# VectorE's share of a softmax exp: one fp16 number from four operations, or a sum of two from three

## The chip, the cores and the metric

The kernel runs on one core of a Trainium2 chip. Times are device microseconds (us) of one execution. The engines are PE (TensorE), ACT (ScalarE), DVE (VectorE) and POOL (GpSimd); "PEld" is PE's weight load.

## The reference, cut to what matters

The program does two independent attention blocks, A (linear attention) and B (full softmax attention), each with S = 2048, D = 512, 32 heads of 16. B is the heavy one:

```
q, k, v = split(x @ wqkv)                   # 32 heads of 16
p = softmax(q @ k.T * 0.25)                 # 32 x 2048 x 2048 exps
o = p @ v
out_b = merge_heads(o) @ wo
```

The kernel works on P transposed (keys on partitions, queries along the columns). It cuts the 32 x 2048 x 2048 scores into 2048 "blocks" of 128 partitions by 512 columns of work for one instruction. V has a column of ones, so the denominators come out of the same product. There are 32 "units" of 64 blocks; a unit is 512 queries of four heads.

## The kernel before

A planner in Python places every instruction before the program is emitted. It knows an assumed duration for each and decides block by block whether ScalarE or VectorE makes the exp. ScalarE reads scores from five PSUM banks (PSUM is where TensorE leaves its results) in turns of 3 and 2 blocks:

```python
# ScalarE: exp of 3 or 2 blocks, PSUM -> fp16                    (L810)
sch.add("act", lambda e: e.activation(PT[:, row, c0:c0 + w], SCR[sl][:, 0:w], ACTF.Exp, scale=SC), ...)
# TensorE refills those banks: QK (q times k) with 32 rows, four row groups   (L664)
e.matmul(dst, lhsT=KM[32*g:32*g+32, ...], rhs=QT[32*g:32*g+32, ...], tile_position=(32*g, 0))
```

VectorE has two further PSUM banks, pD, which it shares with all other work of the kernel. It scales a block and writes it as int16, so that the bits, read as fp16, are 2^n(1+f), a line between powers of two. Then four operations over a group of four blocks correct the mantissa:

```python
DG, NDG = 4, 4              # blocks in a group, groups in flight
DI = sb("DI", [128, NDG, DG * 512], I16);  DQ = sb("DQ", [128, 1, DG * 512], I16)
e.tensor_scalar(DI[...], DB[...], ESC, EB, op0=mult, op1=add)        # L750, 1 block, out of PSUM
tensor_scalar(Dq,  I,   0x200, 6, bitwise_xor, logical_shift_left)   # L866, 2048 columns
tensor_tensor(Dqb, Dq,  Dq,  mult)                                   # L867
tensor_scalar(Dqh, Dqb, EC, EO, mult, add)                           # L868
tensor_tensor(I,   I,   Dqh, add)                                    # L869
```

TensorE multiplies finished blocks with V (L923). These products have 17 output rows and four column groups; the planner charges them so:

```python
while len(bt) < PVB and any(byg.values()): ...     # PVB = 8 blocks at most in a batch
dur = 0.13 + 0.085 * len(bt)                       # the planner's duration, us
e.matmul(PVb[32*g:32*g+17, 0:512], lhsT=VV[:, j, ...], rhs=P, start=first, stop=last_, tile_position=(0, 32*g))
```

## Time and profile before

The kernel before took 831.24 us (median of 3; 829.41 to 832.32). The profiled execution took 834.9 us, longer than all of these. The head of its page, then the two lines of its costliest groups. A group line gives line, engine, operation, output and input tile, shape and count; then busy us and the mean ns of one; then the idle time just before them and what ended most of it.

```profile
span 833.1 us, 12897 instructions
## 1 busy us (share of the span) xinstructions
PE 695.8 (84%) x5406; PEld 210.7 (25%) x5406; DVE 748.5 (90%) x1153; ACT 789.1 (95%) x730; POOL 46.5 (6%) x43
...
PEclk9999999999999799998786999999988998699996
...
ACT 69%; PE 16%; DVE 14%; issue 1%; POOL 0%; POOLq 0%
...
L810 ACT ACTIVATE PT<-pS 128x1536 f16<-128x1536 f32 (+1 forms) x673 | 778.7, 1384 | 23.1 <-PE pD L664 11.2
L664 PE MATMUL pS<-QT,KM 32*128 32x512 bf16 x1682 | 277.5, 410 | 104.3 <-ACT PT L810 100.0
```

And VectorE's part of a block, from the groups kept apart by shape:

```profile
L750 DVE TENSOR_SCALAR DI<-pD 128x512 int16<-128x512 f32 x348 | 234.0, 682 | 29.3 <-PE pD L664 27.2 <-PE pS L664 0.3
L869 DVE TENSOR_TENSOR DI<-DI,DQ 128x2048 int16<-128x2048 int16 x91 | 111.3, 1223 | 1.6
L867 DVE TENSOR_TENSOR DQ<-DQ 128x2048 bf16<-128x2048 int16 x91 | 111.1, 1221 | 1.5
L866 DVE TENSOR_SCALAR DQ<-DI 128x2048 int16<-128x2048 int16 x91 | 63.6, 699 | 1.8
L868 DVE TENSOR_SCALAR DQ<-DQ 128x2048 f16<-128x2048 bf16 x91 | 62.4, 685 | 0.4
```

How to read it. ScalarE is busy 95% of the span, and most of the chain that ended last is its exp. Consecutive exps overlap in the records (the mean of one is longer than busy time over count), so the cost of a block is busy time over blocks: 778.7 / 1682 = 0.463 us. VectorE's cost of a block is 0.682 + (699 + 1221 + 685 + 1223) / 4 / 1000 = 1.64 us. Neither engine can be relieved alone: the time falls when blocks move from ScalarE to VectorE. ScalarE idles 833.1 - 789.1 = 44.0 us.

One line is PEclk, the granted clock in tenths for 40 slices. The mean was 0.924.

### The profile page before, as it was taken

How to read it: one execution, taken by the hardware profiler on the slowest of the kernel's cores; microseconds unless marked ns; L12 is line 12 of the kernel's file. 1: busy time of each engine (PE TensorE's matmuls, PEld its weight loads, DVE VectorE, ACT ScalarE, POOL GpSimd, SP SyncE). 2: the span in 40 equal slices, each digit the busy share in tenths (PEclk: the TensorE clock that was granted, in tenths of full speed). 3: DMA queues.
4: the chain of work that ended last, by engine and by line, in shares of the span. 5: the costliest groups of instructions: out<-in, count | busy, mean ns of one | idle time of the engine just before them, and what ended most of it. 6: DMA issues, size and time to landing. Idle time of an engine off the chain costs nothing.

```text
span 833.1 us, 12897 instructions
## 1 busy us (share of the span) xinstructions
PE 695.8 (84%) x5406; PEld 210.7 (25%) x5406; DVE 748.5 (90%) x1153; ACT 789.1 (95%) x730; POOL 46.5 (6%) x43
## 2 busy tenths in 40 slices
PE   7888888888888888877778889888878888888886
PEld 4322222233222222221111222222222222122222
DVE  6999899986999899899999998999999988999981
ACT  5799999999999999999999999999999999999993
POOL 2000023100000002110000001220000000000000
PEclk9999999999999799998786999999988998699996
DMA  9100000000000000000000000000000000000000
GB/s 307 48 1 24 29 1 1 1 1 1 2 1 1 1 1 1 1 1 1 1 1 1 7 14 7 1 7 14 7 1 14 14 13 13 1 20 14 20 26 29
DMA packets 13136, 13.47 MB, mean 16 GB/s; under 512 B 1808, under 2 KB 12560, under 8 KB 13072
## 3 DMA queue, kind: packets, MB, share of 16 engines
q1 hardware_dynamic: 12272, 12.19, 4.5%
q8 instruction: 44, 0.72, 0.4%
q10 hardware_dynamic: 800, 0.39, 0.2%
q14 instruction: 20, 0.16, 0.1%
HBM read 8.39 MB, written 4.19 MB: 15 GB/s over the span
## 4 chain that ended last, share of the span: by engine, by line
ACT 69%; PE 16%; DVE 14%; issue 1%; POOL 0%; POOLq 0%
ACT PT L810 67%; PE pS L664 5%; PE pPV L923 5%; DVE DI L750 4%; DVE DQ L867 2%; DVE DI L869 2%; ACT EA L534 1%; DVE DQ L866 1%; PE pD L450 1%; PE pD L947 1%; DVE DQ L868 1%; PE pD L615 1%; DVE OT L944 1%; PE pD L543 1%; PE pD L970 0%
## 5 line engine op out<-in xcount | busy, mean ns | idle before, releaser
L810 ACT ACTIVATE PT<-pS 128x1536 f16<-128x1536 f32 (+1 forms) x673 | 778.7, 1384 | 23.1 <-PE pD L664 11.2
L664 PE MATMUL pS<-QT,KM 32*128 32x512 bf16 x1682 | 277.5, 410 | 104.3 <-ACT PT L810 100.0
L750 DVE TENSOR_SCALAR DI<-pD 128x512 int16<-128x512 f32 (+1 forms) x357 | 244.9, 695 | 32.6 <-PE pD L664 30.6
L923 PE MATMUL pPV<-PT,VV 128*17 128x512 f16 x1682 | 220.9, 410 | 0.7 <-ACT PT L810 0.3
L664 PEld LDWEIGHTS pS<-QT,KM 32*128 32x128 bf16 x1682 | 64.6, 91 | 365.0 <-ACT PT L810 325.0
L664 PE MATMUL pD<-QT,KM 32*128 32x512 bf16 x366 | 142.6, 415 | 1.3 <-DVE DI L750 1.1
L869 DVE TENSOR_TENSOR DI<-DI,DQ 128x2048 int16<-128x2048 int16 x92 | 112.0, 1217 | 1.6
L867 DVE TENSOR_TENSOR DQ<-DQ 128x2048 bf16<-128x2048 int16 x92 | 111.8, 1215 | 1.5
L923 PE MATMUL pPV<-DI,VV 128*17 128x512 f16 x366 | 79.7, 425 | 3.0 <-DVE OT L944 2.4
L476 POOL TENSOR_SCALAR KM<-KR,PAR 128x512 bf16<-128x512 bf16 x24 | 41.7, 1748 | 511.3 <-DVE KR L474 511.3
L866 DVE TENSOR_SCALAR DQ<-DI 128x2048 int16<-128x2048 int16 x92 | 64.0, 696 | 1.8
L868 DVE TENSOR_SCALAR DQ<-DQ 128x2048 f16<-128x2048 bf16 x92 | 62.8, 683 | 0.4
L923 PEld LDWEIGHTS pPV<-PT,VV 128*17 128x17 bf16 x1682 | 40.8, 88 | 84.5 <-issue 75.4
L543 PE MATMUL pD<-Wa,xTa 128*128 128x256 bf16 x256 | 39.0, 283 | 4.5 <-DVE DI L750 2.8
L450 PE MATMUL pD<-xTb,Wb 128*128 128x512 bf16 x124 | 37.8, 401 | 5.7 <-DVE DI L750 2.9
L664 PEld LDWEIGHTS pD<-QT,KM 32*128 32x128 bf16 x366 | 31.9, 92 | 10.2 <-DVE DI L750 4.1
L947 PE MATMUL pD<-identf,OT 128*128 128x128 f32 x128 | 31.2, 336 | 1.9 <-DVE OT L944 1.5
L534 ACT ACTIVATE EA<-pD 128x256 bf16<-128x256 f32 (+1 forms) x48 | 30.2, 630 | 0.6 <-PE pD L564 0.6
L944 DVE COPY OT<-pPV 128x512 f32<-128x512 f32 x32 | 21.9, 684 | 8.6 <-PE pPV L923 8.5
L543 PEld LDWEIGHTS pD<-Wa,xTa 128*128 128x128 bf16 x256 | 21.2, 100 | 21.2 <-issue 7.0
L419 DVE CAST OB<-pD 128x512 bf16<-128x512 f32 x30 | 20.5, 683 | 5.2 <-PE pD L615 5.1
L923 PEld LDWEIGHTS pPV<-DI,VV 128*17 128x17 bf16 x366 | 16.3, 90 | 28.5 <-issue 12.5
(88 smaller groups left out, 376.2 us busy)
## 6 DMA issues: line engine op xcount, KB each, us to landing
out_dram<-OB SPq DMA_DIRECT2D x32, 128.0 KB, 1.7
KNa<-in_A_x_dram SPq DMA_DIRECT2D x4, 512.0 KB, 6.1
ON<-in_B_x_dram SPq DMA_DIRECT2D x3, 512.0 KB, 7.7
Wa<-in_A_wqkv_dram SPq DMA_DIRECT2D x1, 1536.0 KB, 11.9
Wb<-in_B_wqkv_dram SPq DMA_DIRECT2D x2, 384.0 KB, 8.4
Wb<-in_B_wqkv_dram SPq DMA_DIRECT2D x1, 512.0 KB, 6.8
WOb<-in_B_wo_dram SPq DMA_DIRECT2D x1, 512.0 KB, 12.0
WOa<-in_A_wo_dram SPq DMA_DIRECT2D x1, 512.0 KB, 12.1
```

The source lines that it names most:

```text
L450: return e.matmul(f32v(bk), lhsT=Wb[:, cc, kind * 512 + Gp * 128:kind * 512 + Gp * 128 + 128], rhs=xTb[:, cc, sc * 512:(sc + 1) * 512], st ...
L476: st.append(("pool", 0.7, f_op("pool", lambda e, e_=e_: e.tensor_scalar(KM[:, r, e_, cs], KR[:, kr, :], PAR[:, e_:e_ + 1], None, op0=ALU.m ...
L543: return e.matmul(f32v(bk)[:, 256 * k_:256 * k_ + 256], lhsT=xTa[:, cc, t * 128:(t + 1) * 128], rhs=Wa[:, cc, 512 + 512 * k_ + 256 * hp:51 ...
L664: return e.matmul(dst, lhsT=KM[32 * g:32 * g + 32, Gp % 2, e_, j * 128:(j + 1) * 128], rhs=QT[32 * g:32 * g + 32, Gp % 2, c * 512:(c + 1) ...
L750: sch.add("dve", lambda e: e.tensor_scalar(DI[:, buf, i * 512:(i + n) * 512], DB[:, bi * 512:(bi + n) * 512], ESC, EB, op0=ALU.mult, op1=A ...
L810: sch.add("act", lambda e: e.activation(PT[:, row, c0:c0 + w], SCR[sl][:, 0:w], ACTF.Exp, scale=SC), reads=skeys(sl), writes=[("PT", row, ...
L866: (0.07 + w * 0.00027, lambda e: e.tensor_scalar(Dq, I, 0x200, 6, op0=ALU.bitwise_xor, op1=ALU.logical_shift_left), ik, [("DQ", q)]),
L867: (0.07 + w * 0.00053, lambda e: e.tensor_tensor(Dqb, Dq, Dq, op=ALU.mult), [("DQ", q)], [("DQ", q)]),
L868: (0.07 + w * 0.00027, lambda e: e.tensor_scalar(Dqh, Dqb, EC, EO, op0=ALU.mult, op1=ALU.add), [("DQ", q)], [("DQ", q)]),
L869: (0.07 + w * 0.00053, lambda e: e.tensor_tensor(I, I, Dqh, op=ALU.add), ik + [("DQ", q)], ik)]
L923: sch.add("pe", lambda e, g=g, j=j, h=h, P=P, first=first, last_=last_: e.matmul(PVb[32 * g:32 * g + 17, 0:512], lhsT=VV[:, j, vcol(h):vco ...
L947: return e.transpose(f32v(bk)[:, qb * 128:(qb + 1) * 128], OT[:, ob, qb * 128:(qb + 1) * 128], identf[:])
```

## The change

The intent is a cheaper block on VectorE, paid on TensorE. The masked bits give two fp16 numbers, H = 2^n(1+f) times (1+f)/2, which is 2^n(1+f)^2/2, and 2^n itself (with a small constant in the mantissa). Their sum is close to a constant times 2^(n+f). The sum is never formed: both are multiplied with V, and TensorE's accumulation adds them. That is three operations on a group instead of four. Both tensors must now live until the product, so DQ grows from 4 to 15 KB a partition. With DI the two grow from 20 to 30 KB. 8 KB of that come from two buffers of the output stage, four fifths of which now lie in KNa, a tensor that A needs only for its K side. Groups become 3 blocks, 5 in flight. THRESHOLD_BITS is a bound on the scores, as float bits: above it a general softmax, whose code is not shown here, runs as well. It goes from 9.5 to 9.25.

```diff
-THRESHOLD_BITS = 0x41180000
+THRESHOLD_BITS = 0x41140000
-    DG = 4
-    NDG = 4
+    DG = 3
+    NDG = 5
-    EB = 15.0 * 1024.0 - 7.95374
-    EC = 3.30484893e-4 / 4096.0
-    EO = -79.35798
+    EB = 14754.203187
-        DQ = sb("DQ", [128, 1, DG * 512], I16)
+        DQ = sb("DQ", [128, NDG, DG * 512], I16)
-        ONT = sb("ONT", [128, 5, 512], BF)
-        OB = sb("OB", [128, 5, 512], BF)
+        ONT = sb("ONT", [128, 1, 512], BF)
+        OB = sb("OB", [128, 1, 512], BF)
 ... (out slots 1 to 4 of ONT and OB are views of KNa, after A's last K job)
-  tensor_scalar(Dq, I, 0x200, 6, bitwise_xor, logical_shift_left)
-  tensor_tensor(Dqb, Dq, Dq, mult)
-  tensor_scalar(Dqh, Dqb, EC, EO, mult, add)
-  tensor_tensor(I, I, Dqh, add)
+  tensor_scalar(Q, I, 0x3FF, 0x3800, bitwise_and, bitwise_or)
+  tensor_tensor(Qh, Ih, Qh, mult)
+  tensor_scalar(I, I, 0xFC00, 8, bitwise_and, bitwise_or)
 ... (both Qh and Ih go to the products)
-            while len(bt) < PVB and any(byg.values()):
+            while nmm < PVB and any(byg.values()):
 ...
+                        nmm += len(bt[-1][2])
-            dur = 0.13 + 0.085 * len(bt)
+            dur = 0.13 + 0.085 * nmm
 ... (within a batch, a round over the column groups with the first numbers, then with the second)
```

More of the change, by code (lines that the diff above doesn't have):

```diff
@@ L601, in bass_concat_heads__linear_attn_block__softmax_full_mha__prompt_kernel @@
         stores = []
+        KNf = KNa[:, :, :].rearrange("p (s b) n -> p s (b n)", b=2)
+        ont = lambda o2: ONT[:, 0, :] if o2 == 0 else KNf[:, o2 - 1, :]
+        obf = lambda o2: OB[:, 0, :] if o2 == 0 else KNf[:, o2 + 3, :]
+        ontk = lambda o2: [("ONT", 0)] if o2 == 0 else kst(o2 - 1)
+        obk = lambda o2: [("OB", 0)] if o2 == 0 else kst(o2 + 3)
         def otr_job(src, keys, o2, needs, gives, lane="dve", **kw):
@@ L608, in otr_job @@
             return Job([("pe", 4 * TRB, f_pe(tr, list(keys) + ["identb"])),
-                        (lane, 0.43 if lane == "dve" else 0.6, f_ev(lane, copy_to(lane, lambda: ONT[:, o2, :], lambda bk: bfv(bk, 512)), [], [("ONT", o2)]))],
-                       needs, gives, **kw)
+                        (lane, 0.43 if lane == "dve" else 0.6, f_ev(lane, copy_to(lane, lambda: ont(o2), lambda bk: bfv(bk, 512)), [], ontk(o2)))],
+                       needs + ([("akv", 1, bl) for bl in range(2)] if o2 else []), gives, **kw)
         def omm_job(ab, t, o2, needs, gives, lane="dve", **kw):
@@ L614, in mm @@
             def mm(e, bk, hb):
-                return e.matmul(f32v(bk), lhsT=ONT[:, o2, hb * 128:(hb + 1) * 128], rhs=WO[:, hb, :], start=(hb == 0), stop=(hb == 3))
+                return e.matmul(f32v(bk), lhsT=ont(o2)[:, hb * 128:(hb + 1) * 128], rhs=WO[:, hb, :], start=(hb == 0), stop=(hb == 3))
             def fin(bk):
-                sch.add(lane, lambda e: copy_to(lane, lambda: OB[:, o2, :], lambda bk: f32v(bk))(e, bk), reads=[bk[3]], writes=[("OB", o2)])
-                stores.append(sch.add(out_lanes[o2], lambda e: e.dma_start(out[0][t * 128:(t + 1) * 128, col0:col0 + 512], OB[:, o2, :]),
-                                      reads=[("OB", o2)], queue="sp", force_signal=True))
-            return Job(halves(mm, [("ONT", o2), wkey]) + [(lane, 0.7 if lane == "dve" else 0.6, fin)], needs, gives, **kw)
+                sch.add(lane, lambda e: copy_to(lane, lambda: obf(o2), lambda bk: f32v(bk))(e, bk), reads=[bk[3]], writes=obk(o2))
+                stores.append(sch.add(out_lanes[o2], lambda e: e.dma_start(out[0][t * 128:(t + 1) * 128, col0:col0 + 512], obf(o2)),
+                                      reads=obk(o2), queue="sp", force_signal=True))
+            return Job(halves(mm, ontk(o2) + [wkey]) + [(lane, 0.7 if lane == "dve" else 0.6, fin)], needs, gives, **kw)
         rem = [[list(range(NT)) for g in range(4)] for u in range(NU)]
@@ L813, in ex @@
                     for i, b in enumerate(bl):
-                        pv_ready[b[0]].append((en_ + LAT, b, PT[:, row, c0 + i * 512:c0 + (i + 1) * 512], ("PT", row, sl), (row, sl)))
+                        pv_ready[b[0]].append((en_ + LAT, b, [(PT[:, row, c0 + i * 512:c0 + (i + 1) * 512], ("PT", row, sl))], (row, sl)))
                 push("act", en + LAT, 0, d, ex)
@@ L855, in chain_next @@
                 return
-            buf, q = qwait.pop(0), qfree.pop(0)
+            buf = qwait.pop(0)
+            qfree.pop(0)
             s_ = dgroup["st"][buf]
@@ L859, in chain_next @@
             w = 512 * n
-            I = DI[:, buf, 0:w]
-            Dq = DQ[:, q, 0:w]
-            Dqb = DQ.bitcast(BF)[:, q, 0:w]
-            Dqh = DQ.bitcast(F16)[:, q, 0:w]
+            I, Q = DI[:, buf, 0:w], DQ[:, buf, 0:w]
+            Ih, Qh = DI.bitcast(F16)[:, buf, 0:w], DQ.bitcast(F16)[:, buf, 0:w]
             ik = [("DI", buf, i) for i in range(n)]
+            qk_ = [("DQ", buf)]
             ops = [
-                (0.07 + w * 0.00027, lambda e: e.tensor_scalar(Dq, I, 0x200, 6, op0=ALU.bitwise_xor, op1=ALU.logical_shift_left), ik, [("DQ", q)]),
-                (0.07 + w * 0.00053, lambda e: e.tensor_tensor(Dqb, Dq, Dq, op=ALU.mult), [("DQ", q)], [("DQ", q)]),
-                (0.07 + w * 0.00027, lambda e: e.tensor_scalar(Dqh, Dqb, EC, EO, op0=ALU.mult, op1=ALU.add), [("DQ", q)], [("DQ", q)]),
-                (0.07 + w * 0.00053, lambda e: e.tensor_tensor(I, I, Dqh, op=ALU.add), ik + [("DQ", q)], ik)]
+                (0.07 + w * 0.00027, lambda e: e.tensor_scalar(Q, I, 0x3FF, 0x3800, op0=ALU.bitwise_and, op1=ALU.bitwise_or), ik, qk_),
+                (0.07 + w * 0.00053, lambda e: e.tensor_tensor(Qh, Ih, Qh, op=ALU.mult), ik + qk_, qk_),
+                (0.07 + w * 0.00027, lambda e: e.tensor_scalar(I, I, 0xFC00, 8, op0=ALU.bitwise_and, op1=ALU.bitwise_or), ik, ik)]
             def go(k_, t_):
@@ L873, in r @@
                     sch.add("dve", fn, reads=rd, writes=wr)
-                    if k_ + 1 < 4:
+                    if k_ + 1 < len(ops):
                         go(k_ + 1, en_)
                     else:
-                        qfree.append(q)
+                        qfree.append(0)
                         chain_next()
-                        P = DI.bitcast(F16)
                         for i, b in enumerate(s_["items"]):
-                            pv_ready[b[0]].append((en_ + LAT, b, P[:, buf, i * 512:(i + 1) * 512], ("DI", buf, i), ("d", buf)))
+                            cs = slice(i * 512, (i + 1) * 512)
+                            pv_ready[b[0]].append((en_ + LAT, b, [(Qh[:, cs], ("DQ", buf)), (Ih[:, cs], ("DI", buf, i))], ("d", buf)))
                 push("dve", t_, 1, dur, r)
@@ L908, in pv_cand @@
                 byg[x[1][2]].append(x)
-            bt = []
-            while len(bt) < PVB and any(byg.values()):
+            bt, nmm = [], 0
+            while nmm < PVB and any(byg.values()):
                 for g in sorted(byg, key=lambda g: -len(byg[g])):
-                    if byg[g] and len(bt) < PVB:
+                    if byg[g] and nmm < PVB:
                         bt.append(byg[g].pop(0))
-            dur = 0.13 + 0.085 * len(bt)
+                        nmm += len(bt[-1][2])
+            dur = 0.13 + 0.085 * nmm
             def run(st, en):
-                for x in bt:
-                    _, (u_, j, g), P, pk, src = x
-                    pv_ready[u].remove(x)
+                mms, rnd = [], []
+                for x in bt + [None]:
+                    if x is None or any(x[1][2] == y[1][2] for y in rnd):
+                        for k_ in range(2):
+                            mms += [(y, k_) for y in rnd if k_ < len(y[2])]
+                        rnd = []
+                    rnd.append(x)
+                for x, k_ in mms:
+                    _, (u_, j, g), parts, src = x
+                    P, pk = parts[k_]
+                    end = k_ + 1 == len(parts)
                     h = 8 * Gp + 2 * g + e_
-                    first, last_ = pv_cnt[u][g] == 0, pv_cnt[u][g] == NT - 1
-                    pv_cnt[u][g] += 1
-                    todo[u] -= 1
+                    first, last_ = pv_cnt[u][g] == 0 and k_ == 0, pv_cnt[u][g] == NT - 1 and end
                     sch.add("pe", lambda e, g=g, j=j, h=h, P=P, first=first, last_=last_: e.matmul(
@@ L926, in run @@
                         reads=[pk, ("VV", j, Gp), ("VV1", Gp)], writes=[("PV", g)], accum=("pv", u, g))
+                    if not end:
+                        continue
+                    pv_ready[u].remove(x)
+                    pv_cnt[u][g] += 1
+                    todo[u] -= 1
                     if src[0] == "d":
```

## The prediction

> **What bounds the kernel now.** ScalarE. The page's part 1 has ACT busy 789.1 of 833.1 us, DVE 748.5, PE 695.8. The chain that ended last is 67% ScalarE's exp (L810). The stages view shows it at 96 to 99 us of every 100 between 100 and 800 us. The softmax has 2048 blocks of 128x512. ScalarE takes 1682 of them in 778.7 us: 0.463 us a block. VectorE takes the other 366. In the groups by shape a VectorE block costs 0.682 us for the scaling out of PSUM (L750), plus a quarter of four operations of 2048 columns (699 + 1221 + 685 + 1223 = 3828 ns, so 0.957): 1.64 us. The other VectorE work is about 145 us, and it idles 85 us.
>
> **What the change does.** The chain goes from two TENSOR_SCALAR and two TENSOR_TENSOR on 4 blocks to two and one on 3. The same operations at 1024 columns took 426 and 692 ns, so a line through both widths gives, as an estimate, 562 and 957 ns at 1536: 2081 ns for three blocks, 0.694 a block. I assume that masking with AND/OR runs at the rate that XOR/shift shows here, and that the fp16 product runs at the rate of today's 16-bit products. The Trainium skill's page "VectorE: DVE Perf Modes" (walkthrough of the modes) says that two-tensor operations on packed 16-bit data reach two results a cycle and one-tensor operations four; the two slopes here (0.518 and 0.267 ns a column) agree. A block is then 1.376 us, 16% less.
>
> The out slots move by address only: A's memory is free from about the middle of the run and B's output starts near three quarters. The smaller groups (15 slots in 5 instead of 16 in 4) only alter buffering.
>
> TensorE pays: each VectorE block is multiplied with V twice. In the trace 2048 such products keep PE busy 300.6 us, 0.147 each; about 415 more add 45 to 60 us (estimate). PE has 137 us idle, 100 of it waiting for ScalarE before QK (L664), so it should mostly fit, at about 93% busy.
>
> **On the critical path.** No VectorE time is on it directly: the gain comes only if the planner hands VectorE more blocks. With VectorE's idle kept at 85 us and ScalarE's other work and idle at 54 us:
> T = 1.376 N + 230, and T = 0.463 (2048 - N) + 54, which gives N = 420 and T = 808. I take a few blocks off (the two pD banks and PE get tighter) and add a little ScalarE idle for PE: N about 412, T about 810, 2.5% less.
>
> **What would show it.** Right: L867's group at about 960 ns, the two TENSOR_SCALAR at about 560; 400 to 430 VectorE blocks; products from DI and DQ together twice that number; ACT still 95% busy with about 760 us; PE 90 to 95% busy. Wrong: VectorE blocks staying near 370 with VectorE idle up (banks or groups limit); idle before L810 for PE rising from 23 us to over 40; L750 waiting more for PE than today's 31 us; masks at a slower rate.
>
> **What would make it wrong.** (1) PE becomes the limit: QK behind longer product batches starves ScalarE. (2) Groups come free later, since both tensors are held until the product and total slots fall by one while blocks come faster. (3) The granted clock, 0.924 on average and 0.85 between 400 and 500 us, changes with the load; if it rises, PE fits more easily. (4) The planner's fixed paces (A's jobs spread to a time of 740) leave less to win at the end.
>
> Predicted: 810 us, 797 to 824 eight times in ten; faster by over 2% 0.63, within 2% 0.34, slower 0.03.

## The result, and the profile after

The changed kernel took 803.3 us (median of 4; 802.37 to 805.94), the kernel before 831.41 in the same rounds; the output is correct. The ratio is 0.967, with a 95% interval of 0.9641 to 0.970. The time lies inside the predicted range, and the kernel is faster by more than 2%, as predicted.

The same lines of the changed kernel's page (L810 is now L813, L664 is L667):

```profile
span 802.0 us, 13758 instructions
## 1 busy us (share of the span) xinstructions
PE 701.2 (87%) x5807; PEld 224.1 (28%) x5807; DVE 699.0 (87%) x1224; ACT 769.7 (96%) x716; POOL 46.2 (6%) x43
...
PEclk9999999999999999999999999999999879999997
...
ACT 83%; PE 10%; DVE 6%; issue 0%; POOL 0%; ACTq 0%; POOLq 0%
...
L813 ACT ACTIVATE PT<-pS 128x1536 f16<-128x1536 f32 (+1 forms) x659 | 759.5, 1404 | 10.5 <-PE pS L667 5.9
L667 PE MATMUL pS<-QT,KM 32*128 32x512 bf16 x1647 | 262.1, 392 | 74.0 <-ACT PT L813 69.5
```

And VectorE's groups by shape:

```profile
L753 DVE TENSOR_SCALAR DI<-pD 128x512 int16<-128x512 f32 x387 | 260.2, 683 | 37.5 <-PE pD L667 34.7 <-issue 0.6 <-PE pS L667 0.5
L870 DVE TENSOR_TENSOR DQ<-DI,DQ 128x1536 f16<-128x1536 f16 x133 | 127.5, 958 | 2.2
L871 DVE TENSOR_SCALAR DI<-DI 128x1536 int16<-128x1536 int16 x133 | 74.7, 562 | 0.9
L869 DVE TENSOR_SCALAR DQ<-DI 128x1536 int16<-128x1536 int16 x133 | 74.7, 562 | 2.5
```

The operations cost what the prediction had worked out from two widths: 958 and 562 ns. A block costs 0.683 + (562 + 958 + 562) / 3 / 1000 = 1.38 us. ScalarE has 1647 blocks instead of 1682; VectorE has 401 instead of 366, not the 412 that were expected.

The 31.1 us of span split by ScalarE's account. (The medians differ by 28.1 us; the page before is of a long execution, and which rows that swells is not known.)

| ScalarE | before | after | difference |
|---|---|---|---|
| exp (L810, L813) busy | 778.7 | 759.5 | -19.2 |
| its other work | 10.4 | 10.2 | -0.2 |
| idle | 44.0 | 32.3 | -11.7 |

35 blocks at 0.463 us are 16.2 of the 19.2 us; the other 3 are a slightly shorter time for each block. The last row is what the prediction did not have: it expected ScalarE to wait a little more for a fuller TensorE. It waits less, and the granted clock rose from 0.924 to 0.972.

### The profile page after: what moved, and what is told of

Same layout as the page of the kernel before. It is cut to its first block, busy times and chain, and to the rows that moved or that the text cites. A ratio compares the mean times of both kernels' runs of the same rounds, so it can differ in the third digit from the quotient of the medians.

```text
span 802.0 us, 13758 instructions
## 1 busy us (share of the span) xinstructions
PE 701.2 (87%) x5807; PEld 224.1 (28%) x5807; DVE 699.0 (87%) x1224; ACT 769.7 (96%) x716; POOL 46.2 (6%) x43
## 4 chain that ended last, share of the span: by engine, by line
ACT 83%; PE 10%; DVE 6%; issue 0%; POOL 0%; ACTq 0%; POOLq 0%
ACT PT L813 81%; PE pPV L932 3%; PE pS L667 3%; DVE DI L753 2%; ACT EA L532 2%; DVE DQ L870 1%; PE pD L618 1%; PE pD L448 1%; DVE DQ L869 1%; PE pD L984 0%; DVE DI L871 0%; PE pD L961 0%; PE pD L562 0%; DVE KM L464 0%; DVE xTb L417 0%
## 5 line engine op out<-in xcount | busy, mean ns | idle before, releaser
L813 ACT ACTIVATE PT<-pS 128x1536 f16<-128x1536 f32 (+1 forms) x659 | 759.5, 1404 | 10.5 <-PE pS L667 5.9
L667 PE MATMUL pS<-QT,KM 32*128 32x512 bf16 x1647 | 262.1, 392 | 74.0 <-ACT PT L813 69.5
L753 DVE TENSOR_SCALAR DI<-pD 128x512 int16<-128x512 f32 (+1 forms) x394 | 268.7, 692 | 38.0 <-PE pD L667 35.2
L667 PEld LDWEIGHTS pS<-QT,KM 32*128 32x128 bf16 x1647 | 63.0, 91 | 315.9 <-ACT PT L813 283.2
L667 PE MATMUL pD<-QT,KM 32*128 32x512 bf16 x401 | 144.0, 393 | 2.6 <-DVE DI L753 2.0
L870 DVE TENSOR_TENSOR DQ<-DI,DQ 128x1536 f16<-128x1536 f16 x134 | 128.2, 956 | 2.2
L932 PE MATMUL pPV<-DQ,VV 128*17 128x512 f16 x401 | 101.3, 392 | 0.3 <-DVE OT L958 0.2
L932 PE MATMUL pPV<-DI,VV 128*17 128x512 f16 x401 | 100.4, 389 | 0.0
L869 DVE TENSOR_SCALAR DQ<-DI 128x1536 int16<-128x1536 int16 x134 | 75.1, 561 | 2.5
L871 DVE TENSOR_SCALAR DI<-DI 128x1536 int16<-128x1536 int16 x134 | 75.1, 561 | 0.9
L541 PE MATMUL pD<-Wa,xTa 128*128 128x256 bf16 x256 | 37.5, 275 | 2.1 <-DVE VNa L545 1.4
L667 PEld LDWEIGHTS pD<-QT,KM 32*128 32x128 bf16 x401 | 33.7, 91 | 17.1 <-DVE DI L753 6.5
L958 DVE COPY OT<-pPV 128x512 f32<-128x512 f32 x32 | 21.8, 682 | 10.2 <-PE pPV L932 10.2
L932 PEld LDWEIGHTS pPV<-DI,VV 128*17 128x17 bf16 x401 | 25.9, 91 | 15.1 <-issue 1.3
L932 PEld LDWEIGHTS pPV<-DQ,VV 128*17 128x17 bf16 x401 | 21.8, 88 | 23.7 <-issue 17.4
```

The lines of the kernel that those rows point to most:

```text
L541: return e.matmul(f32v(bk)[:, 256 * k_:256 * k_ + 256], lhsT=xTa[:, cc, t * 128:(t + 1) * 128], rhs=Wa[:, cc, 512 + 512 * k_ + 256 * hp:51 ...
L667: return e.matmul(dst, lhsT=KM[32 * g:32 * g + 32, Gp % 2, e_, j * 128:(j + 1) * 128], rhs=QT[32 * g:32 * g + 32, Gp % 2, c * 512:(c + 1) ...
L753: sch.add("dve", lambda e: e.tensor_scalar(DI[:, buf, i * 512:(i + n) * 512], DB[:, bi * 512:(bi + n) * 512], ESC, EB, op0=ALU.mult, op1=A ...
L869: (0.07 + w * 0.00027, lambda e: e.tensor_scalar(Q, I, 0x3FF, 0x3800, op0=ALU.bitwise_and, op1=ALU.bitwise_or), ik, qk_),
L870: (0.07 + w * 0.00053, lambda e: e.tensor_tensor(Qh, Ih, Qh, op=ALU.mult), ik + qk_, qk_),
L871: (0.07 + w * 0.00027, lambda e: e.tensor_scalar(I, I, 0xFC00, 8, op0=ALU.bitwise_and, op1=ALU.bitwise_or), ik, ik)]
```

## The experiments

Two theories stood for the smaller idle time. **Theory A**: the extra products keep TensorE from being granted a halved clock. With a slow TensorE the QK fill comes late, and ScalarE waits. **Rival B**: the shorter chain and the new plan let ScalarE wait less, and the extra products are only a cost. "Half-clock time" below is worked out from the page: the records of the granted clock have only the values 1.0 and 0.5 in all these traces, so it is 2 x (1 - clock) x span. The run a0 is the changed kernel once more.

| run | VectorE blocks | clock (profiled) | half-clock us | ScalarE idle us | median us | ratio to before (95%) |
|---|---|---|---|---|---|---|
| before | 366 | 0.924 | 127 | 44.0 | 831.4 | |
| after | 401 | 0.972 | 45 | 32.3 | 803.3 | 0.967 (0.9641 to 0.970) |
| e1_before_twice | 366 | 0.954 | 77 | 47.1 | 840.5 | 1.0135 (1.0059 to 1.0211) |
| e2_after_once | 401 | 0.944 | 90 | 34.4 | 807.5 | 0.9726 (0.9653 to 0.9799) |
| e3_before_groups3 | 369 | 0.922 | 130 | 43.8 | 834.8 | 1.0067 (1.0005 to 1.0129) |
| e4_after_groups4 | 390 | 0.965 | 57 | 35.6 | 812.0 | 0.9771 (0.9699 to 0.9844) |
| a0_after_again | 401 | 0.970 | 48 | 30.6 | 802.1 | 0.9677 (0.9644 to 0.9709) |
| e7_after_cap366 | 366 | 0.957 | 71 | 33.9 | 821.6 | 0.9924 (0.9875 to 0.9972) |
| e8_before_filler | 366 | 0.972 | 46 | 35.2 | 821.9 | 0.9901 (0.9874 to 0.9927) |
| e5_after_charge1 | 412 | 0.978 | 35 | 35.0 | 806.5 | 0.972 (0.9704 to 0.9736) |
| e9_after_filler | 401 | 0.984 | 25 | 25.5 | 800.1 | 0.9656 (0.9575 to 0.9737) |
| e10_after_plan | 409 | 0.982 | 29 | 26.1 | 795.3 | 0.9609 (0.9523 to 0.9696) |
| e11_after_plan_filler | 409 | 0.981 | 30 | 29.7 | 795.8 | 0.9579 (0.9497 to 0.9662) |
| e12_once_filler | 401 | 0.978 | 35 | 26.0 | 798.3 | 0.9631 (0.9551 to 0.971) |

The runs e1 to e4 shared one chip; a0, e5, e7 and e8 a second; e9 to e12 a third. Clock and idle are of the profiled run of each kernel; the median is of all its timed runs.

The record has the clock of every execution, not only of the profiled one. A straight line through a kernel's executions on one chip gives 2 to 6 us less time for each 0.01 of clock, with one exception: on the chip of a0, e5, e7 and e8 the kernel before took 829.0 to 831.3 us at clocks of 0.919 to 0.934, with no trend. The mean clock alone does not set the time, and that the two go together does not say which is the cause.

### What the traces say of the halved clock

First an observation that needed no run. The view by stretches, for two of the half-clock stretches of the kernel before and one full-clock stretch (columns: the stretch; its length; busy us of PE, PEld, DVE, ACT and POOL with instruction counts; clock; DMA share and GB/s):

```profile
437.20:440.60 3.40, 3.40 (x25) 0.54 (x21) 3.40 (x6) 3.09 (x4) 0.00 (x0) 0.50 0.00 0
444.00:454.20 10.20, 9.96 (x53) 2.20 (x55) 9.09 (x14) 8.71 (x8) 0.00 (x0) 0.50 0.01 2
537.00:604.00 67.00, 56.09 (x442) 15.88 (x442) 65.33 (x102) 67.00 (x62) 6.42 (x4) 1.00 0.03 9
```

In the 67 us at full clock ScalarE does not idle at all. In the 10.2 us at half clock it idles 1.5 us, while PE is busy throughout. Laying ScalarE's records over all clock records of the trace, without the first 40 and the last 25 us, gives: before, ScalarE idles 17.0 us, 13.3 of them in 109 us of half clock; after, 6.5 us, 5.3 of them in 34 us. So 8.0 us of the 11.7 us go with the half-clock stretches. That is a coincidence in time, not yet a cause.

The timeline of the kernel before shows the change of speed inside one such stretch; after the start and the length in us, each row has engine, line and tiles:

```profile
436.73 0.39 PE L664 MATMUL pS<-QT,KM 32*128 32x512 bf16 x3 [0.95 <-ACT PT L810]
...
439.50 0.61 PE L664 MATMUL pS<-QT,KM 32*128 32x512 bf16 x3
...
440.16 6.88 ACT L810 ACTIVATE PT<-pS 128x1536 f16<-128x1536 f32 x6 [0.31 <-PE pD L664]
...
441.66 0.39 PE L664 MATMUL pS<-QT,KM 32*128 32x512 bf16 x3 [0.55 <-ACT PT L810]
```

Three QK products of one shape take 0.39 us, then 0.61, then 0.39 again, and ScalarE's 0.31 us wait for TensorE falls into the slow part.

### e1: the products doubled, without the change (wrong)

The batch loop of the changed kernel is put into the kernel before, and a VectorE block is handed to it twice. The plan is not told.

```diff
-  pv_ready[b[0]].append((..., P[:, buf, ...], ("DI", buf, i), ("d", buf)))
+  pv_ready[b[0]].append((..., [(P[:, buf, ...], ("DI", buf, i))] * 2, ("d", buf)))
 ...
+                        nmm += 1            # planned as one
```

> The kernel before, same plan and order (366 VectorE blocks), but each VectorE block is multiplied with V a second time (366 more 17x512 products, not charged in the plan; those blocks then count double, so the result is wrong on purpose). Theory A (the extra products keep TensorE busy, its clock is halved less often, ScalarE waits less): granted clock up from 0.92 to 0.95 or more, time in half-clock stretches down from 126 us to under 80, ScalarE idle down from 44 to about 36 us, time 822 to 827. Rival B (ScalarE's smaller idle came from the shorter chain and the new plan; products only cost): clock and ScalarE idle unchanged or worse, time 831 to 845.

Measured: the half-clock time fell from 127 to 77 us in the profiled run, as theory A has it. But ScalarE's idle time rose from 44.0 to 47.1 us and the kernel became 1.35% slower, as rival B has it. The same overlay as above shows why both hold: idle at full clock rose from 3.6 to 9.0 us, idle at half clock only fell from 13.3 to 12.0. The executions show the cost at an equal clock: at 0.939 e1 took 843.2 and 843.8 us, the kernel before on the same chip 824.4. The likely reason, not traced product by product, is that products that the plan has no room for stand before QK fills that ScalarE waits for. Each half of theory A has to be tested apart.

### e2: the second product taken out of the changed kernel (wrong)

```diff
-  [(Qh[:, cs], ("DQ", buf)), (Ih[:, cs], ("DI", buf, i))]
+  [(Qh[:, cs], ("DQ", buf))]
-                        nmm += len(bt[-1][2])
+                        nmm += 2 if bt[-1][3][0] == "d" else 1     # still planned as two
```

> The changed kernel, same plan and order (401 VectorE blocks, still charged for two products), but only the first of the two numbers is multiplied with V (401 products fewer; wrong on purpose). Theory A: granted clock down from 0.97 to 0.93-0.95, ScalarE idle up from 32 to about 38-42 us, time 808 to 813, slower although work was taken away. Rival B (TensorE's extra products cost something): time 797 to 803, ScalarE idle 32 or less.

Measured: the clock fell to 0.944, within what theory A expects; ScalarE's idle rose to 34.4 us only, short of its 38 to 42. Less work made the kernel no faster: 807.5 us. It is 4 us above the changed kernel, but the two intervals (0.9653 to 0.9799 and 0.9641 to 0.970) overlap, so "slower" is not shown. Rival B's 797 to 803 us were not met either, so nothing here supports that the products cost several us in this plan.

### e3 and e4: the grouping alone, the chain alone

e3 is the kernel before with `DG = 3, NDG = 5`; e4 is the changed kernel with `DG = 4, NDG = 3`.

> The kernel before with groups of 3 blocks in 5 buffers (old chain of four operations). A block costs by the widths 0.682 + (562 + 957 + 562 + 957)/3 = 1.70 us instead of 1.64. The plan gives VectorE 369 blocks (366 before). If the grouping is a gain of its own: under 826. If it only serves the new chain: 829 to 836.

> The changed kernel with groups of 4 blocks in 3 buffers (the room for both tensors does not hold 4 buffers of 4). A block's chain costs (699 + 1222 + 699)/4 = 0.655 us instead of 0.694, but the plan gives VectorE only 390 blocks instead of 401, for want of free groups: 11 x 0.463 / 1 = 5 us more ScalarE work. Expected 806 to 811. If the wider operations matter more than the number of groups: 803 or less.

e3 took 834.8 us: small groups are no gain of their own. e4 took 812.0 us, just above the range. Its chain is cheaper by the block (696 + 1228 + 687 ns for four), yet VectorE waits for blocks twice as long as in the changed kernel (73.2 against 37.5 us):

```profile
L753 DVE TENSOR_SCALAR DI<-pD 128x512 int16<-128x512 f32 x372 | 249.3, 683 | 73.2 <-PE pD L667 68.6 <-PE pS L667 2.8
```

The wait is put down to TensorE, but the plan had sent no block there. Asked without a chip and without regard to memory, the planner gives VectorE 398 blocks with four or more groups of 4, and 390 with three: 8 of the 11 blocks that e4 lacks are lost for want of a free group. In groups of 4 with 3 in flight the new chain wins 2.3%, in groups of 3 with 5 in flight 3.3%. Moving the out slots was not run by itself. The DMA issues of the changed kernel show 16 stores each from OB and from KNa, of 128 KB and 1.7 us to landing for both, as all 32 had before.

### e7: the changed kernel held to the blocks of before

```diff
+    DCAP = 0.1785
 ... in d_pick:
+            if ndv[0] >= 3.5 + DCAP * (NU * UB - sum(left)):
+                return None
```

> The changed kernel, with VectorE held to 366 blocks as before (a cap that grows in step with the blocks taken). ScalarE then has the 1682 blocks of before, 778 us. Theory: the gain comes from two parts, 35 blocks moved (19 of 31 us) and 12 us less ScalarE idle; here only the second is left: 819 to 825 us, ScalarE idle 32 to 36 us. Rival (the shorter chain saves time by itself, the number of blocks is a side effect): under 812. Second rival (it is all the blocks): 829 to 833.

Measured: 821.6 us, with 33.9 us of ScalarE idle, as the theory has it. On this chip the kernel before took 829.4 and the changed kernel 802.1 us. So 19.5 us of the gain need the moved blocks, and 7.7 us come without any block moving (by the interval of e7's ratio, 2 to 10 us). The rival that the shorter chain saves most of the time by itself is out: VectorE is busy only 666.5 us in e7 and waits 75.0 us before the scaling out of PSUM, and the kernel does not gain the time by which VectorE is earlier.

```profile
PE 709.0 (86%) x5772; PEld 222.0 (27%) x5772; DVE 666.5 (81%) x1156; ACT 786.0 (96%) x730; POOL 45.5 (6%) x43
...
L757 DVE TENSOR_SCALAR DI<-pD 128x512 int16<-128x512 f32 x358 | 243.1, 684 | 75.0 <-PE pD L668 71.6 <-issue 0.6 <-PE pS L668 0.5
```

### e8: filler products in the kernel before, result correct

Only where the plan has TensorE idle before a QK fill, up to four products with zero weights are added to sums that are open. They add zero. The plan and the order of everything else are those of the kernel before.

```diff
+            gap = start - T["pe"]
 ...
+                nz = min(4, int(gap / 0.2)) if ... gap >= 0.3 and pvopen[0] is not None ... else 0
+                for i_ in range(nz if gs else 0):          # gs: the column groups with an open sum
 ... (g goes round gs)
+                    sch.add("pe", lambda e, g=g: e.matmul(PVb[32*g:32*g+17, 0:512], lhsT=ZW[:], rhs=WOb[:, 0, 0:512],
+                                                          start=False, stop=False, tile_position=(0, 32*g)), ...)
```

> The kernel before, plan and order unchanged, with 270 products of zero weights (they add zero to the open sums, the result stays right) put only where the plan has TensorE idle before a QK fill. If a halved clock is what makes ScalarE wait: clock up from 0.92-0.93 to 0.945 or more and time down by 3 to 8 us against the kernel before, about 824. Rival (the clock is only a sign of waits, not their cause; TensorE work is a cost): the clock rises, but the time stays within 2 us or grows.

Measured: 821.9 us, 1.0% faster than the kernel before with an interval (0.9874 to 0.9927) clear of 1. TensorE has 270 products more; apart from one memset of the zero weights nothing else changed. These are the lines of this run that answer to those of the kernel before:

```profile
PE 698.3 (85%) x5676; PEld 217.6 (27%) x5676; DVE 746.9 (91%) x1153; ACT 785.8 (96%) x730; POOL 46.5 (6%) x44
...
PEclk9999999999999999998899999999999999999987
...
L822 ACT ACTIVATE PT<-pS 128x1536 f16<-128x1536 f32 (+1 forms) x673 | 776.6, 1417 | 14.4 <-PE pD L666 6.8
```

The clock was 0.967 to 0.977 in the four executions, against 0.919 to 0.934 for the kernel before on this chip. From page to page ScalarE's idle went from 44.0 to 35.2 us. In the overlay used above it idles 8.4 us, 6.1 of them in 38 us of half clock, where the kernel before has 17.0, and 13.3 in 109 us. So 7.2 of the 8.5 us won there lie in the half-clock stretches. The second half of theory A stands: with this plan, filling TensorE's gaps is worth about 8 us, and the gain lies where the clock changed. No run changes the clock and leaves TensorE's work alone, so the clock as the link rests on this overlay. e1 had the same kind of work in the wrong places.

### e5: the plan charges one product where two are made

```diff
-            dur = 0.13 + 0.085 * nmm
+            dur = 0.13 + 0.085 * len(bt)
```

> The changed kernel, with the plan charging TensorE for one product per VectorE block though two are made. The plan then gives VectorE 412 blocks, the number that was forecast, instead of 401. If the missing blocks were lost only to a pessimistic charge: ScalarE does 11 blocks (5 us) less, 797 to 801 us. If the charge was needed: QK fills come late as in the run with doubled products, ScalarE idle over 38 us, 804 to 812.

Measured: 806.5 us against 802.1 for the changed kernel on the same chip; the intervals (0.9704 to 0.9736 and 0.9644 to 0.9709) just touch. The plan did give VectorE the 412 blocks of the prediction, and the exp fell by 4.4 us to 755.2 us; but in the profiled run ScalarE's idle rose by as much, from 30.6 to 35.0 us, short of the 38 us expected. That run took 802.4 us, the shortest of the five; of the other four, 805.9 to 807.1 us, no trace was kept. So the plan's charge for the second products takes the 11 blocks that the prediction had too many, and taking them anyway won nothing.

### e9 and e12: filler with two products and with one

The filler of e8 in the changed kernel, where only 112 products find room, and in e2.

> The changed kernel, plan unchanged, with 112 zero-weight products in TensorE's planned idle (half as many as the kernel before had room for). ScalarE waits only about 5 us in half-clock stretches here, so at most 5 us are to be had: clock up from 0.970 to 0.980-0.988, time 798 to 802. If the clock no longer matters once the real products are there: 801 to 804.

> The changed kernel with one product per VectorE block (wrong on purpose, clock 0.943 and 807 us in the earlier run), plus the same 112 zero-weight products in planned idle. If the second product acts on the time only through the clock, this brings back most of it: clock 0.955 to 0.97, time 801 to 805. If 807 or more: the single product costs time in some other way that is not known.

e9 took 800.1 us at a clock of 0.984: in the expected range, but within the spread of the changed kernel (0.967 to 0.968 on other chips against 0.9656 here). A gain is not shown. e12 bears on the open point of e2. With filler instead of second products the one-product kernel goes from 807.5 us (clock 0.944) to 798.3 us (0.978), below its expected range. That fits the clock as the cause of e2's time, but the two ran on different chips and their intervals overlap (0.9653 to 0.9799 and 0.9551 to 0.971), so it is not shown by these two alone. e12 has 289 products fewer than the changed kernel and no lower a clock (0.970 to 0.978 against 0.964 to 0.974): where the products stand counts, not only how many there are. Beside e9, which differs from it by the second products alone, e12 is 1.8 us faster, less than the spread of either. At nearly equal clocks the second products keep PE's product line (L944 in both) busy 47.6 us longer, 0.119 us each. PE as a whole is busy 34.4 us longer (696.1 against 661.7 us), since part of that time overlaps other matmuls:

```profile
0.00:800.00 800.00, 266.80 (x2449) 60.70 (x2449) 0.98 0.05 17
```

```profile
0.00:800.00 800.00, 219.19 (x2048) 40.47 (x2048) 0.98 0.05 17
```

The first line is of e9, the second of e12; the columns are stretch, length, PE and PEld busy of that source line with counts, clock, DMA share and GB/s.

### e10 and e11: other settings of the planner

```diff
-    PVB = 8
-    DNEXT = 24
-    DEND = 20
-    TEND = 800.0
+    PVB = 6
+    DNEXT = 26
+    DEND = 8
+    TEND = 760.0
```

> The changed kernel with four of the planner's settings changed (at most 6 products in a batch instead of 8, the next unit opened at 26 blocks left instead of 24, VectorE used to the last 8 blocks instead of 20, A's work spread to 760 instead of 800), correct. The plan gives VectorE 409 blocks. If shorter batches let QK fills through in time: 8 blocks x 0.463 = 4 us less, 797 to 800. If shorter batches only cost TensorE more turns: 802 to 808.

> The two before together: 73 zero-weight products and the four settings. If the two add: 794 to 799; if they compete for the same idle of TensorE: as the better one alone.

e10 took 795.3 us, below its expected 797 to 800, and correct, with 409 blocks on VectorE, 26.1 us of ScalarE idle and a clock of 0.982; e11 took 795.8, which both of its expectations allow. Both beat the kernel before clearly, by 3.9 and 4.2%. The changed kernel's median is 7 to 8 us higher, but it was not in the same rounds and the intervals of the ratios overlap, so the step from 803 to 795 is likely rather than shown. The filler adds nothing that can be seen to e10, which has little half-clock time left.

## Why the prediction was right, point by point

- **The bound, and the way the gain comes: right.** ScalarE was the limit and still is (95%, then 96% busy). "No VectorE time is on it directly: the gain comes only if the planner hands VectorE more blocks" holds for 19.5 of 27.3 us (e7 beside a0 and the kernel before). The word "only" was wrong: 7.7 us came with no block moved.
- **The costs of the operations: right.** Foreseen 957 and 562 ns at 1536 columns, measured 958 and 562. The masks run at the rate of XOR and shift: e3 has the old operations at 1536 columns, at 558 and 557 ns with one tensor and 962 and 955 with two. The Trainium skill ("VectorE: DVE Perf Modes", the walkthrough of the modes) says two results a cycle for two-tensor operations on packed 16-bit data and four for one-tensor operations. The slopes between 1024 and 2048 columns (0.518 and 0.267 ns a column) agree, and the new operations lie on them.
- **The blocks: too many.** "N about 412" was 401. The failed step is "with VectorE's idle kept at 85 us": VectorE idles 802.0 - 699.0 = 103.0 us now. Its other work, put at "about 145 us", is 151.9 us (699.0 less 547.1 for the lines of the exp), so that sum was 25 us short. The wait for TensorE before the scaling rose from 30.6 to 35.2 us, which the prediction had listed as a sign of being wrong. e5 shows where the blocks went: a plan that ignores TensorE's second products gives VectorE 412 blocks, and no time is won with them. 11 blocks are 5 us of exp.
- **TensorE: the size right for the products' own line, the sign of its effect wrong.** "Add 45 to 60 us": 47.6 us by e9 and e12, though 34.4 us of all PE's busy time. (The basis of that estimate was loose: it added two group lines that overlap. The view by stretches gives 244.4 us for the 2048 products, not 300.6.) PE was forecast at "about 93% busy"; it is 87%, 701.2 us against 695.8 before. But "add a little ScalarE idle for PE" is the step that failed: idle fell by 11.7 us. What the runs showed in its place: TensorE, with fewer gaps, had a halved clock for 45 us instead of 127, and ScalarE's idle in those stretches fell by 8.0 us. The plan had charged for the work; e1, where it had not, is what uncharged products cost. The prediction named the clock among its doubts ("if it rises, PE fits more easily") and put no number on it.
- **The sum.** With its own 412 blocks the formula gives 811.5 us before any idle is added, so the "about 810" is already below its sum. With 401 blocks it gives 0.463 x 1647 + 54 = 817 us. The measured span is 802, since ScalarE's other work and idle were 42.5 us instead of 54, and a block took 0.461 instead of 0.463 us. Two errors, 5 us too few from too many blocks and more than 11 us too many from idle time, partly cancelled; that the range held owes something to this.
- **Which part of the change raised the clock.** Taking the second products out (e2) lowers it from 0.972 to 0.944; the change as a whole raised it by 0.048. So the products account for about 0.03. The rest, about 0.02, came with the new plan in a way that no run separates.

## What to carry to other kernels

An engine that is not the limit can still hold the limit up through its clock: where TensorE works in bursts with gaps, look at the clock line, lay the bottleneck's idle time over it, and try filler work in places that are idle by plan (e8: 1.0%). Let the schedule know of extra work on a "free" engine: second products that the plan had charged for cost nothing that can be seen (e2, and e12 beside e9), and such products put in without a charge cost 1.35% (e1). When one engine's work gets cheaper, ask how many units of work will really move to it, because the room on a third engine (here TensorE's turns, e5) and the buffers in flight (e4) can decide that.

## What the Trainium skill lacked or had wrong

- "TensorE: Matmul & The Clock Gate", Part 1 and the table "Why this matters for your kernels": the halved clock is told as following an idle window of about 3.4 us, with the advice to leave no gaps over about 3 us between bursts. Its section "A second HAM failure mode: psum-queue depth-cycling" (HAM is its name for the monitor that sets the clock) does tell of a kernel whose clock swings because of short idle times between groups of matmuls, but gives no busy share at which that begins. Here the longest gap without a matmul in the record was 1.56 us (kernel before, without its first 60 and last 25 us), and the clock was halved all the same, in 18 stretches between 40 us and 25 us before the end. The trace (the same part of it) cut into windows of 3.41 us from the start of each full-clock stretch, counted by how busy PE's records were, and how many were followed by half clock:

| PE busy in the window | kernel before | after |
|---|---|---|
| under 0.70 | 33, of which 17 | 8, of which 4 |
| 0.70 to 0.80 | 36, of which 1 | 37, of which 3 |
| over 0.80 | 118, of which 0 | 154, of which 0 |

  So a busy share under about 0.7 already risks it in this kernel. Cut in the same way, e2 and e8 have 16 windows each under 0.70, of which 9 and 6, and 125 and 152 over 0.80, of which 0. It is a risk and no strict rule: about half of the low windows are not followed by half clock, and one window over 0.80 was in each of e1, e9 and e12. The lengths of the stretches, multiples of 3.41 us, and the two values 1.0 and 0.5 agree with the page.
- The same page counts the penalty as lost TensorE time. What it costs an engine that waits for TensorE is not told there: ScalarE idled 13.3 us in 109 us of half clock, and 270 filler products that add zero made the whole kernel 1.0% faster.
- "TensorE: Matmul & The Clock Gate", the row on small-M matmuls: it has 2.38 times for three column tiles, and no figure for four column groups among other matmuls. Here, with 17 rows and 512 columns, one more product cost 0.119 us of the busy time of the products' own line at a clock of 0.98, and 0.086 us of all PE's busy time (e9 beside e12). No single product was timed alone, so a speedup is not given.
